# One order of 2311 operations replaced by another, in a kernel of decayed attention and a bilinear feed-forward block

## The chip, the core and the metric

The kernel runs on one core of a Trainium2 chip. The metric is the device time of one execution in microseconds (us). Three executions of the kernel before took 400.03, 401.91 and 403.84 us; their median, 401.91 us, is the time before.

## The reference

Eight batches of eight heads, 576 positions, 64 wide. Each head has causal attention in which a score gets a decay, the difference of two running sums of log f. The heads' outputs side by side are 4608 tokens of 512 values, which go through a bilinear block with a hidden width of 1536.

```python
scores = scale * np.matmul(q, k.transpose(0, 1, 3, 2))
cum = np.cumsum(np.log(np.clip(f, 0.0001, 1.0)), axis=-1)
decay = cum[:, :, :, None] - cum[:, :, None, :]
scores = np.where(causal, -1000000000.0, scores + decay)
attn = exp(scores - max) / (sum + 1e-09)
x = np.matmul(attn, v).transpose(0, 2, 1, 3).reshape(B * S, H * D)
out = ((x @ w_a) * (x @ w_b)) @ w_out
```

## The kernel before

The program first makes a list of 2311 operations; `op(engines, kind, function, deps)` adds one. An operation is a small group of instructions on one engine: E is TensorE, D is VectorE, A is ScalarE, P is GpSimd and S is the queue of SyncE, which issues transfers. Some operations may go to two or three engines ("DA", "APD"). Then `laid_out` sorts them by a list written out by hand of a search, `ORDER`, and gives each of the 278 that have a choice its letter from `CHOICE`. The loop at the end issues them in that order. So each engine works through its own part of `ORDER` strictly from front to back, and an operation that has to wait holds up all that stand behind it on its engine. How two operations of different engines stand to each other in `ORDER` counts only through the buffers: a pool's buffers are handed out in the order of the list.

The work falls into these kinds.

- **fill**: 40 operations of four 128x128 matmuls on an identity matrix, whose result nobody reads (line 178).
- **Inputs.** `ldqk` and `ldv` load q, k and v of a batch on S into a pool of three buffers (n32). `caqk` and `cav` cast them to 16 bits, and `tqk` (D, line 302) transposes q and k. For batch 0 the halves of q and k are loaded by operations 67 and 75 (k) and 71 and 79 (q); 83 and 84 load and cast the first rows of v. Operations 272 (k) and 275 (q) load the first halves of batch 1.
- **Decay.** `fclip`, `fln`, `fscan`, `fhi`, `flo` make the running sums, `crep` and `cev` spread them over partitions, and `stc` stores them (cum_d).
- **Weights.** `ldw` (line 365) are seven transfers issued by GpSimd: 89 and 90 are the first third of w_a and w_b (512 KB each), 91 and 92 the other two thirds (1 MB each), and 93 to 95 w_out.
- **Attention.** For two pairs of heads at a time: `qk0`, `qk1`, `qk3`, `qk2` (E, line 401) make scores; for batches 0 to 2 `max` (D, line 488) takes maxima, and for the rest `dec` (D, line 512) adds the decay and takes them; `exp` (A, lines 544 and 550), `rec` (D, lines 557 and 559), `norm` (P, line 567). The weights are then turned, in batch 0 by TensorE (`ptr`, line 591), later by a transposing transfer on S (`tr`, line 583), and `pve`, `pv` and `pv4` (E, lines 611 to 636) multiply them with v. The turned weights of rows 384 to 575 lie in a pool of two buffers, PTB: a `tr` into it waits until `pve`/`pv4` of two pairs of heads earlier have read theirs. Batches 0 and 1 are done with `pve` for rows 0 to 255 and for rows 256 to 511.
- **Feed-forward.** In 11 blocks of tokens: `psa` and `psb` (E, line 874), `aev` (A or D, casts psa), `mul` (D, line 890), `pso` (E, line 899), `ocopy` and `sto` (line 914). TensorE's list has these laid between the attention of later batches.

```python
RING = {"S": 2, "bc": 4, "n32": 3, "n16": 2, "PA": 3, "PB": 2, "PTA": 2, "PTB": 2, "st": 8, "ht": 15, ...}
```

Of the kernel before, what the change touches and what calls it, by code (L numbers as in the profile page):

```python
# [37 lines left out]
def kernel(  # L38
# [940 lines left out]
    for t0, n in [(0, 256), (256, 256), (512, 256), (768, 384)] + [(1152 + 512 * n, 512 if n < 6 else 384) for n in range(7)]:  # L979
# [3 lines left out]
        42-44 0 20 41 2 1 64 26 31 23 54 55 45 16 32 13 12 71 46 37 47 56 18 67 27 65 34 72 73 68 48 24 19  # L983
# [3 lines left out]
        142 6 154 155 92 147 143 159 149 91 148 144 160 162 161 108 166-168 145 172 131 52 53 132 179 173 14  # L987
# [42 lines left out]
        831 874 852 1880 875 1829 883 885 1883 1884 1000 884 841 1882 834 880 1885 911 854 857 886 1888-1890  # L1030
        882 814 858 859 849 890 856 891 812 887 912 835 855 1886 819 862 892 1891 864 860 889 888 823 863
        865 893 895 866 896 897 1893-1895 1898 914 881 861 902 898 899 959 960 1892 961 1899 1900 962 1887
        1896 926 927 1901 867 933 868 904 1001 966 934 903 894 901 900 1903 1904 1907 928-930 905 967-969
        1905 1908 813 1014 931 997 1906 815 1911 1909 1910 1912 970 1913 935 915 936 998 919 918 920 963 921
        922 1914 972 937 923 938 973 974 939 1007 940 975 932 971 941 1004 965 976 977 979 978 1915-1918
        1016 1018 1919 924 1921 943 947 916 964 1920 1002 942 994 1008 948 944 980 946 917 909 981 949 1922
        950 1923-1925 945 925 982 1019 952 954 953 1926 955 1015 983 956 913 1927 1928 1931 1932 951 1104
# [4 lines left out]
        1082 1052 1029 1084 1897 1953 1032 1088-1090 1956 1085 1195 1012 1055 1957 1958 1046 1197 1961 1010  # L1042
# [4 lines left out]
        1983 1985 1984 1986-1988 1160 1199 1113 1117 1118 1127 1128 1116 1216 1130 1120 1161 1214 1167 1133  # L1047
# [88 lines left out]
```

## Time and profile before

| | |
|---|---|
| median of three runs (lowest, highest) | 401.91 us (400.03, 403.84) |
| the profiled execution: span from the first to the last instruction | 400.7 us |
| mean granted clock of TensorE | 0.986 |
| busy: TensorE, VectorE, ScalarE, GpSimd | 383.2, 315.3, 250.0, 253.6 us |
| moved by the DMA engines | 78.22 MB |

The profile gives the profiled execution's span; what lies around it can be seen from the runs' median, which is 1.2 us above. PE in the profile is TensorE, DVE is VectorE, ACT is ScalarE, POOL is GpSimd and SP is SyncE (SPq its queue). A row of the timeline has the start, the time taken, the engine, the line, the operation and tiles, and in brackets how long the engine was idle before and what ended that. A row of a table by stretch has the busy time of each engine, then the granted clock of TensorE, the share of the DMA engines and the GB/s.

### The profile page before, as it was taken

Reading aid. Unit: us, or ns where it says so; the run is one execution under the profiler, and the core shown is the slowest. Engines: PE = TensorE matmul, PEld = TensorE weight load, DVE = VectorE, ACT = ScalarE, POOL = GpSimd, SP = SyncE. Lnnn points to the kernel's source line nnn. Section 1 sums busy time; section 2 is a strip of 40 time slices with the busy share of each in tenths; the row PEclk is TensorE's granted clock in tenths of the full one; section 3 lists DMA queues with packets and bytes.
Section 4 is the critical chain, followed back from the end, with each engine's and each line's share of the span. In section 5 each row is a group of like instructions: output and inputs, shape, how many; then the busy total and the mean of one; then the engine's idle time right before and its main releaser. Section 6 shows DMA issues by size and latency. Waiting matters only on the chain.

```text
span 400.7 us, 11076 instructions
## 1 busy us (share of the span) xinstructions
PE 383.2 (96%) x4040; PEld 212.0 (53%) x4040; DVE 315.3 (79%) x907; ACT 250.0 (62%) x757; POOL 253.6 (63%) x424
## 2 busy tenths in 40 slices
PE   8598799998999999999999999999999999999996
PEld 7466576765855544454445454544444444444553
DVE  8989798976778988997988889898969892373560
ACT  5798766666667778758785777577868673300011
POOL 3889876887397876897896849787968553000000
PEclk9889999998999999999999999999999999999999
DMA  7999989989999999999999999999997729000102
GB/s 282 240 186 289 204 177 224 213 150 215 208 301 208 227 171 330 201 277 212 295 187 286 211 255 273 233 241 190 276 187 218 157 66 202 28 2 36 71 0 79
DMA packets 148311, 78.22 MB, mean 195 GB/s; under 512 B 130592, under 2 KB 133408, under 8 KB 148256
## 3 DMA queue, kind: packets, MB, share of 16 engines
q1 hardware_dynamic: 144272, 72.53, 77.4%
q0 software_dynamic: 3696, 4.72, 7.0%
q8 instruction: 31, 0.51, 0.5%
q10 hardware_dynamic: 288, 0.26, 0.2%
q14 instruction: 24, 0.20, 0.1%
HBM read 49.69 MB, written 9.58 MB: 148 GB/s over the span
## 4 chain that ended last, share of the span: by engine, by line
PE 79%; DMA 9%; DVE 4%; POOL 2%; ACT 2%; issue 2%; SPq 0%; POOLq 0%; DVEq 0%; ACTq 0%
PE pso L899 22%; PE psa L874 22%; PE psb L874 21%; PE sc L401 8%; DMA wa<-in_moe_w_a_dram 5%; PE pv L611 2%; DVE st L488 2%; DMA k<-in_k_dram 1%; PE pv L613 1%; PE sc L636 1%; DMA PTB<-spread 1%; DMA PTB<-PB 1%; DVE qT L302 1%; PE pv L623 1%; ACT PB L550 1%
## 5 line engine op out<-in xcount | busy, mean ns | idle before, releaser
L874 PE MATMUL psa<-xT,wa 128*128 128x512 f16 (+2 forms) x528 | 116.2, 343 | 2.3 <-DMA wa<-in_moe_w_a_dram 1.7
L874 PE MATMUL psb<-xT,wb 128*128 128x512 f16 (+2 forms) x528 | 116.2, 343 | 0.1
L899 PE MATMUL pso<-wout,ht 128*128 128x512 f16 (+1 forms) x444 | 98.4, 374 | 0.0
L567 POOL TENSOR_SCALAR PA<-PA,st 128x128 f16<-128x128 f16 (+2 forms) x162 | 76.0, 482 | 31.8 <-DVE st L559 20.4
L890 DVE TENSOR_TENSOR ht<-psb,a 128x512 f16<-128x512 f32 (+2 forms) x132 | 76.2, 589 | 22.0 <-PE psb L874 15.0
L512 DVE CUSTOM_DVE_ANT_0 S<-sc,spread 128x128 f32<-128x128 f32 (+3 forms) x160 | 86.7, 567 | 7.7 <-PE sc L401 5.4
L138 ACT CAST a<-psa 128x512 f16<-128x512 f32 (+2 forms) x85 | 43.5, 515 | 55.9 <-PE psa L874 53.8
L874 PEld LDWEIGHTS <-wa 128*128 128x128 f16 x528 | 50.1, 99 | 45.5 <-issue 3.7
L874 PEld LDWEIGHTS <-wb 128*128 128x128 f16 x528 | 50.4, 99 | 41.5 <-issue 1.7
L567 POOL TENSOR_SCALAR PB<-PB,st 128x512 f16<-128x512 f16 (+1 forms) x84 | 58.7, 712 | 15.7 <-DVE st L559 14.6
L550 ACT ACTIVATE PA<-S,st 128x256 f16<-128x256 f32 (+2 forms) x120 | 59.9, 502 | 12.5 <-DVE st L512 12.4
L899 PEld LDWEIGHTS <-ht 128*128 128x128 f16 x444 | 41.7, 98 | 46.8 <-issue 1.3
L488 DVE TENSOR_REDUCE st<-sc 128x2 f32<-128x512 f32 (+7 forms) x68 | 46.3, 723 | 6.0 <-PE sc L401 5.3
L401 PE MATMUL sc<-kT,qT 32*128 32x128 f16 (+5 forms) x960 | 41.7, 272 | 5.5 <-ACT PA L550 2.1
L550 ACT ACTIVATE PB<-S,st 128x512 f16<-128x512 f32 x40 | 28.5, 714 | 7.9 <-DVE st L512 7.9
L401 PEld LDWEIGHTS <-qT 32*128 32x128 f16 (+1 forms) x960 | 18.6, 96 | 26.7 <-issue 14.4
L142 DVE CAST a<-psa 128x512 f16<-128x512 f32 (+2 forms) x47 | 26.2, 560 | 7.2 <-PE psa L874 6.6
L559 DVE RECIPROCAL st<-st 128x2 f32<-128x2 f32 x128 | 18.5, 157 | 14.0 <-ACT PA L550 8.7
L142 POOL CAST k<-k 128x1152 f16<-128x1152 f32 (+1 forms) x15 | 20.5, 1367 | 8.9 <-DMA k<-in_k_dram 8.9
L138 ACT COPY osb<-pso 128x512 f32<-128x512 f32 (+1 forms) x22 | 12.4, 570 | 19.9 <-PE pso L899 15.1
L138 ACT CAST xT<-pv 128x512 f16<-128x512 f32 (+2 forms) x39 | 17.0, 446 | 11.8 <-PE pv L636 5.8
L140 POOL TENSOR_SCALAR q<-q 128x1152 f16<-128x1152 f32 (+1 forms) x15 | 20.6, 1372 | 5.0 <-DMA q<-in_q_dram 4.2
(98 smaller groups left out, 491.5 us busy)
## 6 DMA issues: line engine op xcount, KB each, us to landing
spread<-cum_d SPq DMA_DIRECT2D x20, 576.0 KB, 5.9
out_dram<-osb SPq DMA_DIRECT2D x35, 256.0 KB, 3.8
q<-in_q_dram SPq DMA_DIRECT2D x15, 576.0 KB, 7.3
k<-in_k_dram SPq DMA_DIRECT2D x15, 576.0 KB, 5.2
v<-in_v_dram SPq DMA_DIRECT2D x32, 256.0 KB, 6.1
wout<-in_moe_w_out_dram POOLq DMA_DIRECT2D x3, 512.0 KB, 8.7
v<-in_v_dram SPq DMA_DIRECT2D x8, 128.0 KB, 7.2
wb<-in_moe_w_b_dram POOLq DMA_DIRECT2D x1, 1024.0 KB, 13.5
```

The costliest lines, as they stand in the source:

```text
L138: nc.scalar.copy(out=out_, in_=in_)
L140: ENG[e].tensor_scalar(out=out_, in0=in_, scalar1=0.125, scalar2=1.0, op0=MUL, op1=MUL)
L142: ENG[e].tensor_copy(out=out_, in_=in_)
L401: nc.tensor.matmul(out=dst, lhsT=lhsT, rhs=rhs, start=start, stop=stop, skip_group_check=True)
L488: nc.vector.tensor_reduce(out=m if i == 4 else st[:, 2 * i:2 * i + 2][:, h:h + 1] if isinstance(x, list) else m, in_=y, axis=AXX, op=MAX, ...
L512: nc.vector.tensor_tensor_reduce(out=o, in0=x, in1=y, scale=-1.0, scalar=3e38, op0=ADD, op1=MIN, accum_out=m)
L550: nc.scalar.activation(out=p_blocks(t, i)[:, :, h, :], in_=x.rearrange("p (j k) -> p j k", k=128), func=EXP, scale=sign, bias=st[:, c:c + ...
L559: nc.vector.reciprocal(out=st[:, 20 + 2 * i:22 + 2 * i], in_=st[:, 10 + 2 * i:12 + 2 * i])
L567: ENG[e].tensor_scalar(out=p, in0=p, scalar1=st[:, c:c + 1], scalar2=1.0, op0=MUL, op1=MUL)
L874: nc.tensor.matmul(out=o, lhsT=w16[:, db, 128 * fb:128 * fb + 128], rhs=tokens(db, t0, n), start=(db == 0), stop=(db == 3))
L890: nc.vector.tensor_tensor(out=ht[:, 0:n], in0=T.pop(("psb", t0, fb))[:, 0:n], in1=T.pop(("a16", t0, fb))[:, 0:n], op=MUL)
L899: nc.tensor.matmul(out=o, lhsT=T[("ht", t0, fb)][:, 128 * tb:128 * tb + 128], rhs=wout16[:, fb, c], start=(fb == 0), stop=(fb == 11))
```

## The change

`ORDER` and `CHOICE` are replaced; no operation, buffer or pool is added, removed or resized. 2214 of the 2311 places of `ORDER` hold another operation than before, but much of that is a shift. On TensorE the sequence of all `psa`, `psb` and `pso` is the same as before; of its 571 places 209 differ, through attention operations and `fill` that stand elsewhere. 105 operations change engine.

```diff
     ORDER = """
-        42-44 0 20 41 2 1 64 26 31 23 54 55 45 16 32 13 12 71 46 37 47 56 18 67 27 65 34 72 73 68 48 24 19
-        69 75 57 58 61 62 49 74 79 76 77 11 70 78 50 66 25 36 51 80 5 96 275 9 276 109 115 81 33 59 110 83
...
+        0 27 18 24 6 39 42 43 40 37 10 1 64 28 31 44-46 3 20 34 54 23 55 17 66 25 47 56 67 68 48 49 12 69 70
+        36 50 71 72 51 65 73 74 57 58 26 79-81 96 75 76 97 98 103 105 59 7 109 110 115 5 77 116 61 62 60 4
...
     CHOICE = """
-        DPAADDAAPPAPAAPADPADDAAADADDDDDAADDDDAAADAAADDAAAADAAAAADAAAAAADAAAAAADDAAADADADDAAAAAADDAAAAAAAAA
...
+        APDDAPAAPPAAPPPAAPPDDDAADDDAAADAADDADAAADAADAAAAAADDADDAAAAAAAADAAAADAAADADAAADDAAAAAADADAAADAADAA
...
```

Read engine by engine, the places on which the prediction rests are these (kind and number of the operation, in order):

```text
S before   ldf42 ldqk71 ldqk67 ldqk75 ldqk79 ldqk275 ldv83 ldv278 ldv85 ldqk272 ldv87 stc63 ldqk280 ...
S after    ldf42 ldqk67 ldqk71 ldqk79 ldqk75 ldv83 ldqk275 stc63 ldv85 ldqk272 ldqk280 ldv278 ldv87 ...
P before   const0 caqk72 caqk68 flo49 caqk77 pad66 caqk276 cav84 norm119 norm120 norm114 norm113 ldw89
           norm101 norm102 ldw90 norm107 cav279 norm138 ldw92 ldw91 ...
P after    const0 pad66 caqk68 flo49 caqk73 flo58 caqk76 caqk77 cav84 ldw89 norm120 norm119 ldw90
           norm114 norm113 caqk276 ldw91 (eight norms) ldw92 norm108 norm107 norm127 norm126 cav86 caqk273 ...
D before   ... fscan47 fscan56 fhi48 fhi57 flo58 tqk74 tqk70 tqk78 max109 max115 caqk81 tqk82 ...
D after    ... fscan47 fscan56 tqk70 cev51 tqk74 max97 max103 max109 max115 tqk82 tqk78 ... cev53 ...
E before   qk2 379, pv4 256, pv4 270, psa, fill, psb ... psa, qk0 464, pv4 426, pv4 417
E after    pv4 256, qk2 379, psa, psb, fill, pv4 270, psa ... psa, pv4 426, qk0 464, pv4 417
E before   pso, pve 424, pve 440, pve 422, pso, pso, qk3 466, pso x3, qk2 467, pv4 444, pve 431, pve 442
E after    pso x3, pve 424, pve 431, pve 440, qk3 466, pso x3, qk2 467, pv4 444, pve 422, pve 442
S before   ... tr438 tr437 ldv460 tr428 tr429 sto1655 tr439 tr430 ldqk603 tr526 ...
S after    ... sto1655 ldv460 tr428 ldv462 tr437 tr419 tr439 tr438 ldqk603 tr430 tr429 tr524 ...
```

`tr` 421 and 412 write the PTB buffers that `pv4` 426 and 417 read; `tr` 439 writes the one that `pv4` 444 reads, and waits for `pve` 424.

More of the change, by code (lines that the diff above doesn't have):

```diff
@@ L1032 @@
[L1032 to L1036, printed above, removed]
@@ new lines @@
+        317 1647 328 329 350 446 447 334 399 448 1648 1651 336 335 395 287 324 371 449 318 450 451 377 1652
+        319 1653 211 1654 330 331 396 1649 708 710 378 268 346 269 353 457 360 307 254 255 250 351 251 354
+        400 15 1656 1657 13 362 361 363 364 35 8 355 356 1660 458 1658 1661 313 325-327 1659 1662 1663 256
+        379 380 257 1664-1667 29 386 270 382 271 1668 1670 381 383 1669 1671 337 1672 1674 1673 1676 352
[3 rows of a table added]
+        1700 1702 1701 365 420 411 415 416 1703 465 480 1704-1706 508 320 481 424 1655 482 314 471 460 390
@@ new lines @@
+        456 391 332 339 483 510 509 511 338 428 431 333 462 437 499 440 441 432 477 466 384 514 515 486 487
+        1709-1711 459 467 419 516 425 488 409 1707 439 444 1712 422 423 453 490 518 624 438 442 443 445 1714
+        1716 492 491 493 1715 603 1718-1720 1722 385 405 519 430 520 506 1717 1721 463 358 500 1723 473 359
+        1724-1726 1728 472 1727 521 1729 429 433 434 528 540 435 436 541 1730 1732 546 548 547 1731 479 1734
+        1733 478 1736 1735 1738 1739 484 485 524 568 574 501 1737 1740 1742 1744 507 1743 517 1746 512 513
@@ new lines @@
+        526 569 575 576 489 1741 549 1748 1747 494 495 525 542 523 570 522 527 461 1749-1751 577 529 532 533
[4 rows of a table added]
+        671 679 673 678 566 567 672 1783-1785 589 596 639 595 680 645 674 675 598 1788 1789 1786 1790 594
+        681 609 640 647 1787 597 1792 682 1791 641 612 613 1793-1796 646 648 610 1798 1797 1800 1802 599 631
[3 rows of a table added]
+        616 661 662 666 665 667 625 697-699 628 1821 1822 1825 668 1826 716 700 701 800 658 761 769 663 1823
+        706 696 728 735 729 629 1771 669 730 737 731 763 762 764 1827 1828 1830 736 738 739 670 1831 704
@@ new lines @@
+        1832 1835 1837 1836 702 768 770 703 1838 615 802 617 771 803 772 1839 1840 705 717 707 721 724
+        732-734 1824 1841 741 720 718 719 773 725 1842 775 740 777 776 722 723 778 774 765 766 742 744 816
+        743 779 781 1843 1833 780 1844 1845 726 782 767 783 715 1847 745 746 749 750 1849 748 806 1848 807
+        1850 1846 1851-1853 784 1854 711 727 747 754 755 820 821 817 818 804 1855 1856 1859 751 752 1857 787
+        788 753 785 756-758 760 1861 1860 1862 1863 1858 824 869 790 789 791 836 837 844 1864 1867 1868 870
@@ new lines @@
+        1865 1866 759 786 808 792 793 1869-1871 1873 838 846 843 809 1872 876 1874 1834 810 877 1875 1876
+        811 1879 805 822 839-842 1877 1878 796 794 906 795 845 825 871 879 872-874 878 828 1881 847 849 797
+        826 829 814 815 832 848 830 831 833 850 851 853 883 884 999 1000 875 996 910 1829 1880 852 827 1883
+        907 885 880 881 854 855 1884 812 834 1882 1885 890 891 886 887 823 892 857 858 893 856 902 859
+        1888-1890 1886 860 835 819 862 864 1893 1894 1887 863 865 1895 1898 1899 895 897 1891 866 896 914
@@ new lines @@
+        898 899 926 933 934 928 888 882 889 904 911 1900 1903 1905 1904 1901 861 959 961 935 967 1892 927
+        966 929 1001 867 868 960 903 894 1906 968 1907 1908 901 1909 1911 1912 1896 1913 969 962 900 997 998
+        908 1910 813 915 918 930 932 905 1014 1016 919 963 964 922 1002 1914 936-938 920 921 970 923 1007
+        973 974 1915 931 939 1917 1018 940 941 976 975 977 1916 1919 1921 965 1918 942 943 1004 924 971
+        947-949 912 979 978 972 1920 1923 1015 944 1925 1924 909 980 916 917 946 981 950 1926 925 945 982
[4 rows of a table added]
@@ new lines @@
+        1028 1031 1048 1012 1025 1045 1050 1081-1084 1049 1078 1079 1051 1951 1952 1198 1953 1032 1080
+        1954-1956 1010 1957 1958 1006 1055 1052 1046 1040 1056 1017 1047 1085 1959 1961 1088-1090 1057 1054
+        1033 1021 1897 1029 1071 1199 1960 1106 1053 1100 1060 1061 1091 1072 1962 1963 1087 1109 1058 1093
+        1966 1967 1094 1062-1064 1112 1095 1124 1125 1131 1092 1073 1212 1086 1066 1096 1097 1099 1968 1971
+        1972 1126 1964 1132 1157 1165 1969 1102 1159 1167 1098 1065 1164 1166 1973 1975 1977 1133 1158 1160
@@ new lines @@
+        1976 1979 1059 1974 1978 1195 1110 1981 1980 1982-1984 1987 1988 1103 1127 1134 1011 1196 1985 1986
+        1013 1117 1120 1989 1128 1130 1101 1113 1116 1118 1161-1163 1129 1121 1168 1170 1202 1203 1990 1135
+        1136 1205 1206 1171-1173 1114 1138 1139 1991 1993 1992 1174 1175 1994 1122 1115 1145 1146 1140 1176
+        1141 1142 1144 1178 1970 1107 1995 1179 1119 1147 1148 1996 1999 1177 1997 2000 2003 1998 1965 1123
+        1111 2001 2002 1150 1151 2004 1180 1216 1218 1200 1217 2005 1183 1184 1152 1181 1153 1214 1154
@@ new lines @@
+        2007-2010 1143 2011 2012 1220 2006 1395 1137 2013 1186 1185 1187 1204 1169 1392 1265 1267 2014-2016
+        1149 1190 2017 2019 1272 2018 2020 2021 2024 1192 1266 1213 1232 1234 1156 1240 1233 1235 2025 2026
+        1155 1191 1207 1182 1189 1188 1274 1273 1239 1396 1397 1241 1221 1236 1237 1224 1193 1225 1226 2022
+        1201 1238 1228 1242-1245 2027 1229 1246 1268 1269 1271 1247 1275 1276 1278 1302 1248 1279 1280 2029
+        2030 1249 1281 1277 1250 1251 1282 1283 1285 1208 1284 2028 1222 1223 1270 1252 1303 1230 1286 1253
@@ new lines @@
+        1287 1219 1306 1307 1227 1288 1254-1257 2031 2034 2023 2035-2037 1231 1298 1289 2032 1291 1293 1292
[10 rows of a table added]
+        1423 1504 1399 1474 1476 1407 1422 1500 1467 1469 1424-1427 1444 1475 1477 1479 1478 2096 1468 2099
[7 rows of a table added]
+        1569 1532 1574-1576 1571 2140 2143 2145 1572 2144 2147 1541 1542 2142 1577 2146 1533 1503 1519 1546
[3 rows of a table added]
+        2179 2180 2183 2181 2182 2184-2187 2189 2188 2191 2193 2190 2192 2195 2197 2194 2196 2199 2159 2198
+        2201 2200 2202 2203 2205 2204 2207 2209 2208 2211 2210 2174 2213 2212 2214-2217 2219 2218 2220 2221
@@ L1086 @@
+        2206 2223 2222 2224-2226 2228-2237 1594 1597 1588 1591 2238-2240 2243 2244 2247 2245 2246 2249 2248
+        2250 2251 2253 2241 2252 2255 2254 2256-2260 2263 2261 2262 2264 2265 2267 2266 2227 2269 2268
+        2271-2273 2275 2276 2270 2277 2278 2274 2242 2279-2284 2287 2288 2285 2291 2292 2286 2289 2290 2293
+        2296 2294 2295 2297 2298 2301 2299 2300 2302-2310
     """
     CHOICE = """
-        DPAADDAAPPAPAAPADPADDAAADADDDDDAADDDDAAADAAADDAAAADAAAAADAAAAAAADAAAAAADDAAADADADDAAAAAADDAAAAAAAAA
@@ L1089 @@
-        AAADDDAADADDAAAADDADDDDDADAADDADDADADAAAADAAADADAADAAAADAAAAAADDDAAAAAADADAAAAAAADAADAAAAAADAAAAADA
-        AADAAADADAAADAADAAAAAAAAAADDAAADAAADDAAAAAADAAAAADDADDDDDADDDDADDDDAADADDDAADAAA
+        APDDAPAAPPAAPPPAAPPDDDAADDDAAADAADDADAAADAADAAAAAAADDADDAAAAAAAADAAAAADAAADADAAADDAAAAAADADAAADAADAA
+        DDDDAAAADDDDADADDDAADDAADDDDDADDDADDADDDADDDAADDDDAAAAAAAAAAADAADAAADAAAAADAAADAAAAAAAAADDDAAAAAAAAD
+        DDAAAADDADAAAAAAAAAAAAAAADADAADAADAAAAAADADAADDDADAAADDDDDDADDDDADAAADAAAADAAS
```

33 lines of the change are left out of this document (3 added, 30 removed), and 109 rows, old and new, of the table ORDER.

## The prediction

> **What bounds the kernel now.** I read the page first, then tables by stretch, then the waits of TensorE, and then the timeline around each wait.
>
> ```profile
> span 400.7 us, 11076 instructions
> ...
> PE 383.2 (96%) x4040; PEld 212.0 (53%) x4040; DVE 315.3 (79%) x907; ACT 250.0 (62%) x757; POOL 253.6 (63%) x424
> ...
> PE   8598799998999999999999999999999999999996
> ```
>
> TensorE is busy for all but 17.5 us of the span. Since the change leaves its operations alone, what can be won is idle time, half-clock time and small stalls. The last row has TensorE's busy tenths in 40 slices of 10 us: from the eleventh on each digit but the last is a 9. There the new list can win little, and can lose. The tables by stretch say where these lie.
>
> ```profile
> 8.00:20.00 12.00, 6.67 (x151) 4.87 (x151) 11.62 (x25) 8.38 (x33) 10.20 (x22) 0.88 0.99 265
> 20.00:32.00 12.00, 11.05 (x178) 8.29 (x176) 10.44 (x25) 9.89 (x35) 10.16 (x18) 0.83 1.12 196
> 32.00:44.00 12.00, 8.85 (x174) 6.74 (x172) 11.44 (x31) 10.19 (x35) 11.01 (x16) 1.00 1.10 277
> 44.00:78.00 34.00, 33.76 (x554) 24.88 (x558) 30.91 (x69) 23.88 (x75) 25.20 (x40) 1.00 1.01 204
> 92.00:106.00 14.00, 11.78 (x199) 9.52 (x192) 8.16 (x20) 8.78 (x30) 8.58 (x13) 0.88 1.16 201
> ```
>
> The columns after the length are PE, PEld, DVE, ACT, POOL, clock, DMA share. From 8 to 44 us VectorE is the fullest engine (33.50 of 36), and TensorE waits. So the case is decided in the first 106 us, by these waits:
>
> ```profile
> PE sc L401 <- ACT PA L550: 2.1, 1, 2.1
> PE sc L401 <- DVE st L559: 2.1, 1, 2.1
> PE pv L636 <- DMA PTB<-spread: 1.8, 1, 1.8
> PE psa L874 <- DMA wa<-in_moe_w_a_dram: 1.7, 1, 1.7
> PE pv L636 <- DVE st L488: 0.8, 1, 0.8
> ```
>
> The first two are score matmuls ahead of 20 us that wait for the softmax to give up their buffers. They are not all recoverable, since VectorE is full there.
>
> **The first 20 us.** VectorE loses three pieces of work and gains one:
>
> ```profile
> 6.99 0.49 DVE L142 CAST wout<-cum_f 32x256 f16<-32x256 f32 x2
> 7.52 1.03 DVE L220 TENSOR_TENSOR wout<-cum_f,wout 32x320 f16<-32x320 f32 x1
> 12.65 1.16 DVE L140 TENSOR_SCALAR q<-wout 128x512 f16<-128x512 f32 x1
> 28.95 0.40 DVE L142 CAST xT<-pv 128x256 f16<-128x256 f32 x1
> ```
>
> The two fhi go to ScalarE (0.49), flo 58 to GpSimd (1.03), the cast 81 of q to ScalarE (1.16); both cev of 256 columns come to VectorE, whose nearest row is the cast at 28.95 (0.40 each). Net 0.49 + 1.03 + 1.16 - 0.80 = 1.9 us less on the fullest engine. ScalarE and GpSimd have the room (8.38 and 10.20 of 12). **I count 1.9 us**; the bounds are 0, if another queue takes over, and 4.2, both waits.
>
> **The weights.** The 1.7 us are the wait for the second part of w_a:
>
> ```profile
> 14.43 1.04 POOL L142 CAST nv<-v 128x1024 f16<-128x1024 f32 x1 [0.90 <-DMA v<-in_v_dram]
> 17.05 0.98 POOL L365 DMA_DIRECT2D wa<-in_moe_w_a_dram  x1
> 22.51 0.75 POOL L365 DMA_DIRECT2D wa<-in_moe_w_a_dram  x1
> 22.51 21.65 DMA wa<-in_moe_w_a_dram
> 44.21 0.61 PE L874 MATMUL psa<-xT,wa 128*128 128x256 f16 x4 [1.65 <-DMA wa<-in_moe_w_a_dram]
> ```
>
> It is issued last of four at 22.51 and lands 21.65 us later. From 20 to 32 us the two queues shared the transfer engines thus:
>
> ```profile
> q0 software_dynamic: 1505, 1.97, 98.1%
> q1 hardware_dynamic: 625, 0.35, 13.5%
> cum_d<-cum_f SPq DMA_DIRECT2D x1, 144.0 KB, 11.0
> ```
>
> GpSimd's queue had 98% of them and moved 1.97 MB in 12 us; SP's small store of the sums took 11.0 us. In the new list w_a's second part goes ahead of w_b's, two norms and a cast after ldw 90. Also v is loaded before batch 1's q, into the third free buffer, so cast 84 needn't wait till 14.43 and the first issue comes up to 4 us sooner. At 1.97 MB in 12 us the 2.1 MB up to its end take 12.8 us: counted from 20 us it lands near 33 instead of 44. w_b's second part, now last, needs 6.4 us more at that rate, 13 if SP's queue takes half: 39 to 46, less up to 4 for the sooner start, against the 42.6 (44.21 - 1.65) at which TensorE asks now and 40.7 with the gain above. **I count 1.65 us**; bounds 0 and 1.65. It is hidden again if GpSimd's norms ahead of the issues come late.
>
> The Trainium skill ("DMA: Bandwidth & Descriptors", the section on queues, rings and completion order) says that each engine goes round the queue rows packet by packet; even shares would make about 21 us of the 2.1 MB (half of the 2.3 MB that all queues moved in 12 us), so w_a's second part would land at 41 and w_b's after it. The 98.1% against 13.5% speak against even shares here, though SP had little queued; the sum above goes by the row.
>
> **The transposes.** The 0.8 us are laid to VectorE, but the wait is for a transposing transfer. Below are the chain, SP's queue from 69 us on, the landings of these two transposes and of all, and TensorE:
>
> ```profile
> 66.43 0.44 PE psa L874 x4
> 68.68 1.08 PE sc L401 x26
> 69.76 0.43 PE pv L636 x20
> ...
> 70.19 6.36 SPq L583 DMA_TRANSPOSE PTB<-PB  x2
> ...
> DMA to landing us min/median/max: 6.0/6.4/6.9
> ...
> DMA to landing us min/median/max: 2.8/4.4/7.2
> ...
> 78.27 0.35 PE L636 MATMUL pv<-PTB,nv 128*64 128x64 f16 x10
> 79.45 0.35 PE L636 MATMUL pv<-PTB,nv 128*64 128x64 f16 x10 [0.84 <-DVE st L488]
> ```
>
> pv4 256 and 270 free both buffers at 70.19; tr 421 and 412 are issued at 70.2 and 73.4 (half of 6.36 later) and land 6.9 and 6.0 us later, at 77.1 and 79.4. The second is the 0.84. TensorE's work between the release and pv4 426 was 78.27 - 70.19 = 8.1 us. The new list moves qk2 379, a psa, a psb and a fill (1.08 + 0.44 + 0.44 + half a psa = 2.2 us) from behind the release of pv4 256 to before that of 270, for which tr 421 now waits: the lead shrinks to 5.9. With the same landings the first waits 1.0 and the second (9.2 us after the release, wanted after 7.0) 2.2 in all instead of 0.84. With the median landing of 4.4 neither waits. **I count 0.5 us lost**, bounds 1.4 lost and 0.84 won.
>
> ```profile
> 84.96 4.37 SPq L583 DMA_TRANSPOSE xT<-spread  x2
> 90.06 3.54 SPq L583 DMA_TRANSPOSE PTB<-spread  x2
> 90.06 4.18 DMA PTB<-spread
> ...
> 85.60 0.28 PE L623 MATMUL pv<-PTB,nv 128*64 128x128 f16 x4
> 86.14 1.90 PE L899 MATMUL pso<-wout,ht 128*128 128x512 f16 x8
> 94.28 0.35 PE L636 MATMUL pv<-PTB,nv 128*64 128x64 f16 x10 [1.77 <-DMA PTB<-spread]
> 96.00:98.00 2.00, 2.00 (x11) 1.39 (x10) 1.01 (x3) 1.62 (x6) 0.76 (x2) 0.50 0.71 233
> ```
>
> The 1.8 us come from order in SP's queue: pve 424 frees the buffer at 85.9, but tr 439 stands behind tr 428, tr 429 (4.37 together) and a store and is issued at 90.06; it lands 4.18 later. The new list puts it before 429, with the store long gone. TensorE's work between 424 and 444, 92.5 - 85.9 = 6.6 us, loses two pso (1.73 at the rate of the row at 86.14): 4.9. Issued at once, a landing of 4.18 fits; tr 438, now behind it, is wanted after a pv4 and a pve more, some 0.7 us later, and lands 1.6 (half of 3.54, rounded down) + 4.4 = 6.0 after the release, 0.4 late. **I count 1.4 us won**, bounds -1.5 (two landings of 6.9) and 1.8.
>
> After that gap the clock is 0.50 for 96 to 98 us; the stretch of 92 to 106 has 0.88 of 14 us, so 3.4 us ran at half, which costs 1.7. **I count half, 0.85**, since any 1.5 us gap may bring it back. The Trainium skill ("TensorE: Matmul & The Clock Gate", the section on oscillation) allows idle gaps up to about 3.4 us without throttling; by it, closing this gap would win no clock. The trace differs: 1.77 us sufficed. The half clock in 16 to 24 us I count at nothing: TensorE isn't the bound there (bounds 0 and 2).
>
> Last, tr 527 waits for pv4 435, which now stands behind qk0 528, a psa and a psb (about 0.9 + 0.44 + 0.44 = 1.8 us less lead; no wait shows there now): **0.3 lost**, bounds 0 and 1.5.
>
> **Sum.** 1.9 + 1.65 - 0.5 + 1.4 + 0.85 - 0.3 = 5.0, so a span of 395.7. The runs' median lies 1.2 above the span: 396.9. The last store goes by SP in place of ScalarE, which I leave in the rounding. I forecast **397.0**. The head start of 44 us must be kept until 120: from 44 to 78 us VectorE has 3.1 us of room and GpSimd 8.8, which hides it.
>
> **Rivals.** *Transposes as tight as before* (0.27): the first 44 us win their 3.5, but 421/412, 439 and 527 wait with congested landings, 1.4 + 0 + 1.0 lost and the half clock kept: 400.7 - 3.5 + 2.4 + 1.2 = 400.8; with one of them free 399.5, which I take. For it: the leads shrink in three of four places. Against it: 439's queue is cleared.
>
> *The early gain is not kept* (0.14): VectorE is as full with other work, or GpSimd, which takes flo 58, more casts and waits for caqk 276 ahead of ldw 91, delays the norms by as much; only 439 and the clock change: 400.7 - 1.4 + 0.8 + 1.2 = 401.3.
>
> *Slower* (0.11): the sooner weights starve SP's loads of batch 1. cav 86 and caqk 273 stand right behind ldw 92 on GpSimd, which comes to them near 25 us (22.5 and four norms). If k's load takes the 11 us of cum_d and goes out once the weights flow, at some 17 to 22, it lands at 28 to 33, and all norms of batch 0 that stand behind, which feed the transposes and TensorE, are 3 to 8 us late. Of that 3.5, the early gain gone and one more half-clock window (1.7) give 400.7 + 3.5 + 1.7 + 1.2 = 407, and 405 if 439 still wins. It decides from an issue at about 14 us on (25 - 11).
>
> *Even shares of the two queues* (0.03): w_a's second part lands at 41 and w_b's later, TensorE waits there as now, and the 1.65 fall away: 398.6. This is what the page named above would give.
>
> **Numbers.** The forecast has the remaining 0.45; its own range is 393.5 to 399. Runs of 400.0 to 403.8 say that a change under 1% (4 us) can't be told from none. Below 397.9 lie 0.36 of the forecast's 0.45 and the better end of the first two rivals, 0.10 (leads that suffice after all): faster 0.46. Slower is 0.12, the slower case and a little of the second. The rest, 0.42, is within 1%. The range of 393.5 to 403 leaves out most of the slower case and a tail of some 0.08 at the fast end.
>
> **What would show it.** Right: the first psa waits no more for wa at about 40 us; TensorE's two waits for score buffers shrink to some 2.3 us together; no gap over 1 us at the pv4 near 75 and 90 us; fewer half-clock windows. Wrong: a wait for PTB over 1.5 us; a GpSimd cast waiting for k near 25 us; any idle of TensorE after 120 us, where I assume that the new list keeps it as busy as now.

## The result, and the profile after

The changed kernel takes **406.07 us** (median of 14 runs, 405.11 to 408.35) against 402.20 us before (14 runs, 400.03 to 404.28). The ratio is **1.0107, with a 95% interval of 1.0084 to 1.0130**: it is 4.3 us slower. The prediction said 397.0, and its range ended at 403.0.

The page of the changed kernel has, for the rows shown of before:

```profile
span 404.0 us, 11033 instructions
...
PE 384.1 (95%) x4040; PEld 212.3 (53%) x4040; DVE 314.0 (78%) x911; ACT 248.9 (62%) x750; POOL 254.5 (63%) x427
...
PE   6698899998999999999999999999999999999996
...
PEclk9559999999999999999999999999999999999999
```

The span is 3.3 us longer. TensorE's idle time is 19.9 us instead of 17.5, and its clock is near half in the second and third slice. In the stages that the prediction used, and in the rest of the attention work (for the changed kernel first, then for the kernel before; the columns are again length, PE, PEld, DVE, ACT, POOL, clock, DMA share and GB/s):

```profile
8.00:20.00 12.00, 6.38 (x135) 4.26 (x133) 8.17 (x20) 9.47 (x30) 7.47 (x12) 0.67 1.10 268
20.00:32.00 12.00, 10.98 (x164) 8.31 (x164) 11.45 (x26) 10.18 (x39) 9.58 (x18) 0.62 1.11 228
...
44.00:78.00 34.00, 32.43 (x539) 24.54 (x539) 29.43 (x68) 26.38 (x81) 27.77 (x42) 1.00 1.07 213
...
92.00:106.00 14.00, 12.91 (x213) 9.86 (x211) 12.32 (x31) 8.75 (x31) 10.28 (x17) 1.00 1.11 181
...
sum 231.00, PE 226.85 PEld 112.06 DVE 197.49 ACT 161.22 POOL 168.59; mean PE 37.81 PEld 18.68 DVE 32.91 ACT 26.87 POOL 28.10
```

```profile
sum 231.00, PE 230.50 PEld 114.42 DVE 199.56 ACT 167.90 POOL 173.32; mean PE 38.42 PEld 19.07 DVE 33.26 ACT 27.98 POOL 28.89
```

Four things are to be read. From 8 to 20 us VectorE has shed 3.5 us (11.62 to 8.17), and TensorE did not become busier for it. From 44 to 78 us TensorE lost 1.3 us of work, from 92 to 106 us it gained 1.1. And in the 231 us from 99 to 330, which the two sums cover, TensorE was idle for 0.5 us before and is for 4.15 now. TensorE's waits say with whom (total, times, longest):

```profile
PE sc L401 <- DVE kT L302: 2.3, 1, 2.3
PE sc L401 <- DVE qT L302: 1.8, 1, 1.8
PE sc L636 <- DMA PTB<-PB: 1.6, 3, 0.8
PE psP L591 <- DVE xT L142: 1.6, 1, 1.6
...
PE pv L623 <- DMA xT<-spread: 1.3, 2, 1.0
...
PE pso L899 <- DMA wout<-in_moe_w_out_dram: 0.8, 1, 0.8
```

All five waits quoted of before are gone, w_a's 1.7 and the 1.8 at `pv4` 444 among them. Others stand in their place.

TensorE's FFN sequence is the same in both kernels, so the start of its k-th matmul instruction (of 1500) measures progress. The table gives the length of the stages in us, worked out from these starts, with lowest and highest of all profiles taken in this study whose code up to the end of the stage is that of the order (of the rear: whose code in the stage is that order's, whatever the front). The lists of e4 and e16 change at FFN matmul 0, so they count in the last row alone; e18, edited near matmul 224 and beyond, counts in the first two.

| stage, to FFN matmul | profile before | profile after | old order, all | new order, all |
|---|---|---|---|---|
| the start, to 0 | 30.4 | 31.8 | 30.4 to 31.2 (5) | 31.5 to 32.6 (7) |
| 0 to 48 | 17.4 | 16.4 | 16.6 to 19.3 (5) | 16.4 to 16.5 (7) |
| 48 to 224 | 39.3 | 39.4 | 38.7 to 39.3 (5) | 39.4 to 39.9 (6) |
| 224 to 260 | 12.4 | 10.1 | 10.0 to 12.4 (4) | 10.1 to 13.3 (3) |
| 0 to 260 together | 69.1 | 65.8 | 65.9 to 69.1 (4) | 65.8 to 69.1 (3) |
| the rear, 260 to 1160 | 230.2 | 235.4 | 230.1 to 233.5 (8) | 235.1 to 237.3 (4) |

Two stages carry the loss, the start with 1.4 us (means 30.6 and 32.0) and the rear with 4.5 us (means 231.6 and 236.1). The rear has the same 2244 matmul records in both orders, so its lengths compare like with like. The three stages between do not: the new list moves eleven `ptr` matmuls from 0 to 48 into the next stage, and 26 of `pve` from there into 224 to 260. Taken together they hold the same work but for four matmuls of fill, and there the means are equal, 67.2 us. The two losses add up to 5.9 us where the runs differ by 4.3; the profiles are few. From 1160 to the last matmul it is 67.5 us in both. The last column but one also shows that the profile of before, on which the sum was built, was a slow one here: it had 12.4 us in a stage that took 10.0 to 11.0 in the three other executions of the same code, and the longest of the four lengths from 0 to 260.

### The profile page after: what moved, and what is told of

It is laid out like the page before. It is cut to its first block, busy times and chain, and to the rows that moved or that the text cites. A ratio compares the mean times of both kernels' runs of the same rounds, so it can differ in the third digit from the quotient of the medians.

```text
span 404.0 us, 11033 instructions
## 1 busy us (share of the span) xinstructions
PE 384.1 (95%) x4040; PEld 212.3 (53%) x4040; DVE 314.0 (78%) x911; ACT 248.9 (62%) x750; POOL 254.5 (63%) x427
## 4 chain that ended last, share of the span: by engine, by line
PE 60%; DMA 11%; DVE 10%; POOL 9%; ACT 4%; issue 4%; SPq 1%; POOLq 0%; ACTq 0%
PE psa L874 17%; PE psb L874 16%; PE pso L899 15%; PE sc L401 6%; DVE st L488 4%; DMA spread<-cum_d 3%; POOL PA L567 2%; DVE S L512 2%; DMA PTB<-PB 2%; PE pv L611 2%; POOL spread L567 2%; DMA k<-in_k_dram 2%; POOL PB L567 1%; DMA xT<-spread 1%; DMA q<-in_q_dram 1%
## 5 line engine op out<-in xcount | busy, mean ns | idle before, releaser
L567 POOL TENSOR_SCALAR PA<-PA,st 128x128 f16<-128x128 f16 (+2 forms) x162 | 75.1, 478 | 42.5 <-DVE st L559 29.1
L138 ACT CAST a<-psa 128x512 f16<-128x512 f32 (+2 forms) x80 | 41.6, 525 | 34.4 <-PE psa L874 32.1
L488 DVE TENSOR_REDUCE st<-sc 128x2 f32<-128x512 f32 (+8 forms) x68 | 46.6, 726 | 12.3 <-PE sc L401 8.0
L142 DVE CAST a<-psa 128x256 f16<-128x256 f32 (+2 forms) x52 | 27.5, 536 | 6.0 <-PE psa L874 5.4
L559 DVE RECIPROCAL st<-st 128x2 f32<-128x2 f32 x128 | 18.6, 157 | 14.1 <-ACT PA L550 9.0
L550 ACT ACTIVATE PA<-sc,st 128x256 f16<-128x256 f32 (+2 forms) x42 | 19.5, 476 | 9.7 <-DVE st L488 9.1
L142 POOL CAST nv<-v 128x1024 f16<-128x1024 f32 (+1 forms) x24 | 21.3, 892 | 3.5 <-DMA v<-in_v_dram 3.5
## 6 DMA issues: line engine op xcount, KB each, us to landing
wa<-in_moe_w_a_dram POOLq DMA_DIRECT2D x1, 1024.0 KB, 11.5
```

The source lines that it names most:

```text
L138: nc.scalar.copy(out=out_, in_=in_)
L142: ENG[e].tensor_copy(out=out_, in_=in_)
L488: nc.vector.tensor_reduce(out=m if i == 4 else st[:, 2 * i:2 * i + 2][:, h:h + 1] if isinstance(x, list) else m, in_=y, axis=AXX, op=MAX, ...
L550: nc.scalar.activation(out=p_blocks(t, i)[:, :, h, :], in_=x.rearrange("p (j k) -> p j k", k=128), func=EXP, scale=sign, bias=st[:, c:c + ...
L559: nc.vector.reciprocal(out=st[:, 20 + 2 * i:22 + 2 * i], in_=st[:, 10 + 2 * i:12 + 2 * i])
L567: ENG[e].tensor_scalar(out=p, in0=p, scalar1=st[:, c:c + 1], scalar2=1.0, op0=MUL, op1=MUL)
```

## The experiments

Apart from the edits shown, all kernels have the same operations. "Old" and "new" are the orders with their choices of engines. Ratios are against the kernel before, with 95% intervals.

**One part alone: w_a's load ahead of w_b's.**

```diff
-        142 6 154 155 92 147 143 159 149 91 148 144 160 162 161 108 166-168 145 172 131 52 53 132 179 173 14
+        142 6 154 155 91 147 143 159 149 92 148 144 160 162 161 108 166-168 145 172 131 52 53 132 179 173 14
```

> The order before, with one thing of the change: the load of the second third of wa (operation 91) stands ahead of that of wb (92) in GpSimd's stream. The wait of 1.65 us for wa at 42.56 should be gone. Theory (the next late arrival takes the place of the wait, as the changed kernel's wait of 1.60 us at 43.16 suggests): the time stays within 0.6 us of before, 401.6 to 402.6. Rival (the forecast's own step, a wait removed is kept to the end): 1.65 us less, 400.5.

Measured: 0.9997 (0.9971 to 1.0023). The wait is gone; of TensorE's waits between 31 and 46 us only 0.3 us concern a weight:

```profile
PE psb L874 <- DMA wb<-in_moe_w_b_dram: 0.3, 1, 0.3
```

The stage 0 to 48 took 16.1 us, and yet the time is the same within 1.2 us (the interval's lower end). The rival's 1.65 us, kept to the end, are outside the interval.

**Front and rear exchanged.** The seam is at FFN matmul 256, operation 1722; in the last kernel at the first one, operation 1598.

```text
e2: new up to 1722, then what is left in the old order      e3: old up to 1722, then what is left in the new order
e4: new up to 1598, then what is left in the old order
```

> The new order up to matrix multiplication 256 of the FFN (start at 98.9 us before, 1.7 us sooner in the changed kernel), then every remaining operation in the old order with the old engines. Theory (the front of the new order gains, its rear loses): the lead of 1.8 us is kept by the old rear, 400.4. Rival (the rear is slow because of what the front leaves behind, late loads and full buffers): no gain is kept, 402 to 406.

> The old order up to the same matrix multiplication, then the rest in the new order. Theory (the rear of the new order loses 5.2 us by itself, from a lead of 1.8 to a lag of 3.4): 402.2 + 5.2 = 407.4. Rival (the rear is harmless behind the old front): 402.2. In between, 404.0, if a part of the rear's loss is only the lead of operations that the new front had drawn ahead of the cut.

> The new order up to the first matrix multiplication of the FFN (30.4 us before, 31.8 after), then the old order. Theory (the new start costs 1.5 us and nothing behind makes up for it): 402.2 + 1.5 = 403.7; its load of wa comes early, so that with that wait's 1.65 us kept it would be 402.0. Rival (the start carries the whole loss, by its half-clock stretch of 17 us and the loads it delays): 405 to 406.

Measured: 1.0113 (1.0070 to 1.0157), 1.0088 (1.0056 to 1.0119) and 1.0215 (1.0183 to 1.0247). The rear alone loses 3.5 us, between the theory's 5.2 and its in-between value. But the new front alone loses 4.5 us instead of gaining 1.8, so the first theory falls; in its profile 2.3 us are lost ahead of FFN matmul 260 and 2.2 behind it. The two kernels lose 8.0 us together, not the 4.3 of the whole, so a seam probably costs something of its own. In e4 one wait of 6.4 us stands behind it, and that kernel tells nothing more.

**The start: engines alone, and everything but the engines.**

```diff
 # e5: ORDER old; in CHOICE nine letters new       # e6: ORDER new; the same nine letters old
-fhi48 D  fhi57 D  flo58 D  caqk81 D  caqk76 A  caqk72 P  caqk73 A  cev51 A  cev53 D
+fhi48 A  fhi57 A  flo58 P  caqk81 A  caqk76 P  caqk72 A  caqk73 P  cev51 D  cev53 A
```

> The order before, with the new engines for nine operations of the start alone: casts 48, 57 and 81 from VectorE to ScalarE, 58 from VectorE to GpSimd, 76 from ScalarE to GpSimd, 72 and 73 exchanged between GpSimd and ScalarE, copies 51 and 53 exchanged between ScalarE and VectorE. The forecast's step (VectorE is the bound of the first 20 us): the first FFN multiplication up to 1.9 us sooner than 30.4 us and a time of 400 to 401. Theory from the changed kernel's trace (the second halves of q and k now come late from ScalarE and GpSimd, the first product with them starts at 16.60 instead of 15.18 us): 1.5 us more, near 403. Nothing measurable, if the new order is needed for either: 401.6 plus or minus 1.

> The new order, with the same nine operations on their old engines. Theory (these engines cost the new start its 1.5 us): 406.0 - 1.5 = 404.5, and a half-clock stretch shorter than 13 us. Rival (the order of the start costs it, not the engines): unchanged, 406. The forecast's step (the new engines gain 1.9 us): slower than the changed kernel, 408.

Measured: 0.9986 (0.9955 to 1.0017) and 1.0233 (1.0178 to 1.0288). In the old order the new engines make the first FFN matmul 1.9 us later (32.5 us against the mean of 30.6), the opposite of the forecast's step: VectorE waits for GpSimd's cast of k, which now stands behind `flo` 58.

```profile
11.49 1.21 DVE L302 STREAM_TRANSPOSE kT<-k 128x576 f32<-128x576 f32 x1 [1.94 <-POOL k L142]
```

The wait for w_a is then missing from TensorE's waits, and the time is the same: w_a lands at 44.6 us here and at 44.2 before, and a weight that lands so late absorbs a late start just as it absorbs an early one. In the new order the old engines are 5 us worse, and the first FFN matmul comes at 35.1 us; there the forecast's step has its sign, and more than its size. So the order alone makes the start later than 30.6 us, the engines alone do too, and together they partly make up for each other.

**The rear: which queue?**

```text
e7: old front; rear of VectorE, ScalarE, GpSimd, SyncE new, of TensorE old      e8: old; only TensorE's rear new
```

> The old order up to FFN multiplication 256 (98.9 us); behind it the new order and engines of VectorE, ScalarE, GpSimd and SyncE, with TensorE's own order left as before. Theory (the rear loses because the maxima, exponentials, normalisations and transposes that feed TensorE come later in their queues): the loss of 3.5 us of the run with the whole new rear stays or grows, 405 to 407. Rival (TensorE's own new order puts its attention work too early): 401.6, as before.

> The old order and engines everywhere, with TensorE's order alone new from FFN multiplication 256 up to 1240 (the last attention work). Rival theory (TensorE's new order is what loses): the 3.5 us of the whole new rear, 405. Theory (the queues of the other engines lose): 401.6, or 402.5 if single products that were moved ahead now wait.

Measured: 1.0242 (1.0191 to 1.0293) and 1.0101 (1.0048 to 1.0155). TensorE's new order alone, behind 99 us, loses what the whole new rear loses (the rear took 234.9 us). The other queues' new order alone loses more. TensorE's waits from 98 to 330 us in e8 are short and have several partners; the longest are these:

```profile
PE sc L636 <- DMA PTB<-PB: 1.0, 2, 0.6
PE sc L401 <- DVE st L512: 0.8, 1, 0.8
PE psa L874 <- DVE a L142: 0.7, 2, 0.5
```

**The rear's single waits, moved away.** TensorE's list alone is edited; old with the swap of e1 in e10.

```diff
 # e9, new order; the same for 433, 631, 1024, 1423
-psb1751 pv4 529 pv4 533 psa1754 qk1 537 psb1755
+psb1751 pv4 529 psa1754 psb1755 pv4 533 qk1 537
 # e10, old order
-pv4 426 pv4 417 psb1689 fill psa1692        qk2 467 pv4 444 pve 431 pve 442 fill fill
+pv4 426 psb1689 psa1692 pv4 417 fill        qk2 467 pve 431 pve 442 fill fill pv4 444
```

> The new order, with five attention products of TensorE's order (433, 533, 631, 1024, 1423: those that wait in the profile at 100, 108, 131, 215 and 301 us, for 0.98, 0.83, 0.56, 0.62 and 0.23 us, mostly for transposes that SyncE has issued 1.4 to 3.6 us before) each put behind two more FFN multiplications. Theory (the rear loses by these single waits, since the transposes land just behind the product): they go, 3.2 us less, 403. Rival (each wait only shows that VectorE, ScalarE and GpSimd are behind as a whole, and comes back at the next product): unchanged, 405.5 to 406.5.

> The old order with the load of wa ahead of that of wb, as before in the swap alone, and with the same edit at its own waits: product 417 (a wait of 0.84 us at 78.61) behind two more FFN multiplications, product 444 (1.78 us at 92.50) behind two other products and two fills that are ready, its eviction moved behind theirs. Theory (a wait that goes is kept, since behind 99 us TensorE hardly waits): 1.0 for the swap, 0.8 and 1.2, 3.0 us in all, 398.7. Rival (given back at the next late buffer, as with the swap alone): 401 to 402.

Measured: 1.0176 (1.0150 to 1.0202), and 0.9983 (0.9961 to 1.0006). Both theories fall. e10's rival holds; e9 is 2.8 us slower than the changed kernel, which its rival did not expect either. In e9 no product waits for PTB any more, but the score products do, for VectorE's maxima to free their buffers, and the rear took 238.9 us:

```profile
PE sc L401 <- DVE st L512: 2.4, 4, 1.1
```

In e10 both old waits are gone; w_b, now last, keeps TensorE for 3.0 us, and another transpose for 1.1:

```profile
PE psb L874 <- DMA wb<-in_moe_w_b_dram: 3.0, 1, 3.0
PE pv L623 <- DMA PTB<-spread: 1.1, 1, 1.1
```

**The half clock of the start.**

```diff
-        for n in range(4):
+        for m in range(LONG.get(n, 4)):    # e11, old order with the swap: LONG = {21: 32}; e12, new order: {26: 28, 2: 36}
```

> The old order with the load of wa ahead of that of wb, and the fill ahead of the first products of batch 0's second heads (operation 21) longer by 28 small multiplications, which occupy the wait of 2.12 us at 13.06. Theory (the half-clock stretch of 6.8 to 10.2 us behind it costs the start): it goes or shrinks, the first FFN multiplication comes 1 us sooner and the swap lets it be kept: 400.5. Rival (TensorE waits for VectorE's casts and maxima there at any clock): 401.6, no change against before.

> The new order with two fills made longer (26 by 24 small multiplications, 2 by 32), in front of the waits of 1.82 us at 8.12 and 2.32 us at 14.28. Theory (the half-clock stretch of 17 us from 12 us on is what delays the new start by 1.5 us): it shrinks to 7 us or less, the first FFN multiplication starts near 30.4 instead of 31.8 us, 404.5. Rival (the start waits for late casts at any clock): the stretch shrinks and the time stays, 406; if the fills outlast the waits, up to 407.

Measured: 1.0044 (1.0020 to 1.0068) and 1.0063 (1.0035 to 1.0091). In the old order neither expectation holds: the half-clock stretches of the start are 10.2 us in all (6.8 before), the first FFN matmul comes at 32.9, and the time is 1.8 us more. In the new order, from 8 to 20 us, the clock is 0.97 instead of 0.67:

```profile
8.00:20.00 12.00, 8.07 (x196) 6.67 (x194) 8.81 (x21) 10.01 (x33) 7.47 (x12) 0.97 1.09 264
```

The half-clock stretch is 10.2 us instead of 17.1, the first FFN matmul starts at 31.4 (mean of the new order 32.0), and the ratio is 0.0044 below the changed kernel's, 1.8 us. The two intervals overlap a little, so this is likely but not certain.

**VectorE and ScalarE made lighter.** e13 and e15 leave the second FFN product out of all but 32 columns, e14 leaves out half of the first, and e17 half of the hidden values.

```diff
 # e13 (new) and e15 (old), tokens from 512 on; q = 32
-tensor_tensor(out=ht[:, 0:n], in0=psb[:, 0:n], in1=a16[:, 0:n])
+tensor_tensor(out=ht[:, 0:q], in0=psb[:, 0:q], in1=a16[:, 0:q]); tensor_tensor(out=ht[:, q:n], in0=a16[:, q:n], in1=a16[:, q:n])
 # e14 (new): the copy out of psa at n // 2 columns          # e17 (new): the multiplication at half its columns
```

> The new order, with VectorE's multiplications of the FFN lightened from the third block of tokens on (token 512 and above, from 97 us on): only the first 32 columns multiply the PSUM product with its partner, the other columns square the fp16 copy, which leaves the second FFN product out of the result and shortens an instruction of 0.68 us. Theory (the rear's waits come from VectorE's queue being late): the waits behind 99 us shrink from 5.4 us to under 1.5, 402. Rival (they come from GpSimd's normalisations and SyncE's transposes): unchanged, 406.

> Control: the old order with the same light multiplication as in the new one. TensorE waits 0.5 us in all behind 99 us there, so that nearly nothing can be gained: 401.5 to 402.3. If it gains 3 us or more, VectorE's length is worth that much in any order, and the run of the new order says nothing about its rear.

> The new order, with the FFN's copies out of PSUM (most of them on ScalarE) at half their columns from token 512 on; the multiplication reads that half twice, so that half of the first FFN product is left out of the result. Theory (VectorE's queue is late, ScalarE's is not): 405, since 12 of the copies in 200 us are VectorE's. Rival (ScalarE's exponentials come late, behind its copies, and VectorE's reciprocals wait for them, 12.4 us of its idle time against 8.8 before): most of the rear's loss goes, 402 to 403.

> The new order, with VectorE's FFN multiplications at half their columns from token 512 on (the third FFN matrix multiplication reads that half for all rows, so that half of the hidden values is left out of the result): a copy of 256 columns out of PSUM took VectorE 0.41 us where the multiplication of 512 took 0.68, so about 17 us less of VectorE's work between 120 and 320 us. Theory (VectorE's queue is what is late in the rear): TensorE's waits behind 99 us, 5.4 us by its starts, fall under 2, and the time is 402 to 403. Rival (transposes in SyncE's queue and GpSimd's normalisations): the waits stay, 405.5 to 406.5.

Measured: e13 1.0186 (1.0147 to 1.0224), e15 1.0063 (1.0034 to 1.0091), e14 1.0123 (1.0081 to 1.0165), e17 1.0133 (1.0091 to 1.0174). The light multiplication was a heavy one, on the mean 182 + 599 ns instead of 684 (from 120 to 320 us, e15):

```profile
L893 DVE TENSOR_TENSOR ht<-a 128x480 f16<-128x480 f16 x53 | 31.8, 599 | 0.0
L891 DVE TENSOR_TENSOR ht<-psb,a 128x32 f16<-128x32 f32 x65 | 11.8, 182 | 4.4 <-PE psb L874 3.1 <-ACT a L138 0.2
```

So the pair tells what 0.1 us more per multiplication costs: 2.5 us in the old order, and 3.2 on top of the new one's loss. The Trainium skill ("VectorE: DVE Perf Modes", the perf-mode tier table) gives a two-input operation of 16-bit data in SBUF twice the rate. The trace agrees for those that ran while GpSimd was idle: 480 columns took 377 to 399 ns. The mean of 599 comes from some that ran beside GpSimd's work and took up to 1590; the last section has both. e17 is shorter for certain:

```profile
L891 DVE TENSOR_TENSOR ht<-psb,a 128x256 f16<-128x256 f32 x53 | 21.7, 419 | 5.9 <-PE psb L874 3.0 <-ACT a L138 2.2
```

That takes 14 us of work off VectorE in these 200 us (53 times 0.265). The rear took 234.2 us, 1.2 less than the changed kernel's profile, and the time is that of the changed kernel within its interval. Lighter copies change nothing that can be seen either. Set against the changed kernel's ratio, the two intervals leave room for a gain of at most 0.9 us (e17) and 1.3 us (e14), so the amount of VectorE's multiplications or ScalarE's copies is not what most of the new rear's 4.5 us come from.

**The middle alone, and one transpose put back.**

```diff
 # e16: old up to 1598, new up to 1722, old behind it
 # e18, new order, SyncE:                                      GpSimd: cav 463 behind the norms 358 and 359
-tr437 tr419 tr439 tr438 ldqk603 tr430 tr429 tr524
+tr437 tr419 tr429 tr439 tr438 ldqk603 tr430 tr524
```

> The old order up to the first FFN multiplication (30.4 us), the new one from there to FFN multiplication 256 (98.9 us), the old one behind it. Theory (the middle gains a little, by the traces so far 0.75 us up to multiplication 48 and 0.55 from 224 to 260, and loses 0.4 between): 401.4. Rival (the middle carries the front's loss, by its new waits at 43 and 60 us): 404 to 406. A seam between two schedules can cost something of its own, as the 6.4 us wait of the run with the new start alone: this would show as one long wait just behind 30 or 98 us.

> The new order, with transpose 429 put back ahead of 439, 438 and 430 in SyncE's queue, as it stood before the change, and GpSimd's cast 463, which waits 3.47 us for a load of v at 85.5, behind the normalisations 358 and 359 that feed 429. Theory (SyncE issues without a break there, so that a wait only changes its place): the wait of 0.98 us at product 433 goes and one of 0.7 to 1.8 us comes back at product 444, and the time stays within 0.7 us of the changed kernel, 405.4 to 406.8. The forecast's step (the new place of 439 gains 1.4 us for good): 407.5. Rival (the cast's wait for v was what made 429 late, and order has nothing to do with it): both products are free of waits, 405.

Measured: 1.0068 (1.0039 to 1.0097) and 1.0207 (1.0167 to 1.0246). e16 reached FFN matmul 260 at 98.4 us, within the 96.3 to 99.4 of the old order, and its rear took 233.5 us, the longest of the old order's; TensorE's longest waits behind the seam are for transposes:

```profile
PE pv L623 <- DMA xT<-spread: 1.1, 1, 1.1
PE pv L623 <- DMA PTB<-spread: 1.0, 1, 1.0
```

In e18 the wait came back at product 444 as expected, yet the other did not quite go, and the clock fell to half behind it:

```profile
96.42 0.35 PE L636 MATMUL pv<-PTB,nv 128*64 128x64 f16 x10 [1.64 <-DMA PTB<-spread]
...
103.64 0.25 PE L623 MATMUL pv<-PTB,nv 128*64 128x128 f16 x2 [0.40 <-DMA PTB<-spread]
```

It is 4.0 us slower than the changed kernel by the ratios, so the theory of an exchange without loss falls, and so does the rival, by which the cast's wait for v made 429 late: with that cast moved away, GpSimd waits at the same place for VectorE,

```profile
89.55 0.93 POOL L567 TENSOR_SCALAR PA<-PA,st 128x256 f16<-128x256 f16 x2 [4.22 <-DVE st L559]
...
91.06 1.21 SPq L583 DMA_TRANSPOSE xT<-spread  x1
92.37 1.50 SPq L583 DMA_TRANSPOSE PTB<-spread  x1
```

and SyncE stands still until 91.06 for the norms of `tr` 429, with `tr` 439 behind it (88.46 in the changed kernel). So in the new order the new place of 439 is worth having, and the forecast's sign holds there. The size is not shown: the 4.0 us hold the move of the cast and the half clock behind the gap as well.

No kernel here beats the one before by more than its interval; e10, at 0.9983, comes nearest.

## Why the prediction was wrong, point by point

**The first 20 us (1.9 won; measured 1.4 lost).** The step summed VectorE's work as if it were the bound. VectorE did get lighter, by 3.5 us, and then stood idle, waiting for ScalarE. One of the two waits that it quotes was also misread: the product at 15.18 in the kernel before came right behind VectorE's transpose of q, which it needs and whose row runs from 13.92 to 15.13, and not behind a score buffer. This is the chain of work that leads to the score product of batch 0's second heads in the changed kernel (start, length, engine, tile):

```profile
7.69 0.88 ACT q L136
8.59 0.61 ACT L202
...
10.09 0.35 ACT wout L138
10.43 1.41 ACT q L136 x2
11.85 0.46 ACT PA L550 x2
12.33 1.03 DVE st L488 x2
13.38 0.57 ACT PA L550 x2
13.98 0.42 DVE st L488
14.40 1.11 DVE qT L302
15.51 1.04 DVE kT L302
16.60 1.40 PE sc L401 x38
```

L202 is the second table load, for the exponential. It took 1.28 us (its row is below) and stands ahead of the cast `fhi` 57 and two casts of q, so that the first exponential begins at 11.75 us. On VectorE the new list has four maxima ahead of the last two transposes, where the old one had two maxima ahead of the last alone, and the maxima wait 0.86 and 0.63 us for exponentials. So the transposes come late, and the product stands at 16.60 against 15.18 before. In the kernel before, the table was loaded ahead of all casts. The load in the changed kernel, then in the kernel before:

```profile
8.59 1.28 ACT L202 ACT_TABLE_LOAD   x1
...
4.90 1.28 ACT L202 ACT_TABLE_LOAD   x1
```

ScalarE "has the room (8.38 of 12)" was true as a share and irrelevant. No run moves the table load or the maxima alone, so how the 1.4 us divide between them is not shown; e5, which loads the table at 4.93 and starts the FFN late all the same, shows that another link can be as slow. One term was also too large: the 1.16 us for the cast 81 of q are a row with GpSimd at work beside it, and in e6 the same cast took VectorE 0.41.

The half clock, counted at nothing in the early start (bounds 0 and 2), is 6.8 to 10.2 us long in the first 30 us of the profiles with the old start and 13.7 to 17.1 us with the new one; e12 prices the part that its fills remove at about 1.8 us, of which 0.5 shows at the first FFN matmul.

**w_a's wait (1.65 won; the wait went, the gain did not come).** The mechanism was right up to the landing: GpSimd issued the load at 20.87 us, it landed 11.5 us later, at 32.4 (the forecast had near 33), and TensorE no longer waits for it. But the sum took a wait that goes for time that is won. In the same stage TensorE now waits as long for a copy by VectorE,

```profile
44.76 0.61 PE L591 MATMUL psP<-ident,PB 128*128 128x128 f16 x8 [1.60 <-DVE xT L142]
```

and its idle time between FFN matmuls 0 and 48 fell only from 3.4 to 3.0 us. The rest by which that stage is shorter is work that the new list does later (14.1 us of matmuls before, 13.3 now). e1 shows that the wait alone is worth nothing measurable.

**`tr` 421 and 412 (0.5 lost).** Neither `pv4` waits now: 0.84 was won, its better bound, if the profile of before is the measure; in three more executions of the old front the wait was 0.75, 0.48 and 0.50 us.

**`tr` 439 and the clock behind it (1.4 + 0.85 won).** In the two profiles compared, this came true (12.4 to 10.1 us). It was mis-sized by taking one execution for the kernel: in three more executions of the old front the wait at 444 was 1.33, 1.38 and 0.46 us and no half clock followed, and e2, with the new front, has a half-clock window near 92 us. TensorE's idle time in the stage is 1.6 us on the mean of four profiles with the old front and 1.0 of three with the new one, so some 0.5 us were won there, and over 0 to 260 nothing. And the wait went on to `pve` 433, for `tr` 429, which now stands last:

```profile
100.09 0.25 PE L623 MATMUL pv<-xT,nv 128*64 128x128 f16 x2 [0.98 <-DMA xT<-spread]
...
108.30 0.35 PE L636 MATMUL sc<-PTB,nv 128*64 128x64 f16 x10 [0.83 <-DMA PTB<-PB]
```

**`tr` 527 (0.3 lost).** The second row: 0.83, inside its bounds.

**Nothing lost behind 120 us (measured about 3.1 lost there, 4.5 from 99 us on).** This term, put at nothing, is the largest error. From FFN matmul 372, at 122 us, to 1160 the old order took 207.8 to 210.2 us (8 profiles, mean 208.8) and the new one 210.8 to 212.4 (4, mean 211.9). The dense rear of the old list was read as a property of the work; it is a property of the list. e3 loses 3.5 us with the new rear alone. e8 shows that TensorE's new order alone suffices for that, and e7 that the other queues' new order does not suit TensorE's old one. e9, e14 and e17 speak against three simple causes: five badly placed products, ScalarE's copies, the length of VectorE's multiplications. What stays open is which of TensorE's moved products begins it: the waits are 0.2 to 1.0 us each, on several partners, and moving five of the products only led to other waits.

**The rivals.** By its number "slower" (407, or 405) was the nearest, by luck: its mechanism was loads starved by the weights, and no cast waiting for k near 25 us shows. By mechanism "the early gain is not kept" was nearer, with 401.3 and a chance of 0.14; but it laid the blame on VectorE or GpSimd, and it still counted 439's gain. Of the signs that the prediction named, w_a's wait, the gaps near 75 and 90 us went its way; the score waits (1.8 and 2.3) did not shrink, the half-clock stretches grew, and TensorE is idle after 120 us, its own sign of being wrong.

## What to carry to other kernels

A stage that is full to the last microsecond is not safe from a new order: price a rewritten list there as a loss with a bound, not as zero. A busy share does not say what a freed engine is worth; follow the chain of the first late operand through each engine's queue, table loads included. When two orders are compared by stages, count the work in each stage first. Before a wait of one profiled execution enters a sum, ask whether another execution of the same code shows it, and what lands next if it goes.

## What the runs showed of the hardware that I had not expected

The half-clock stretches come in steps of 3.41 us (6.8, 10.2, 13.7 and 17.1 us in these profiles) and begin elsewhere in each execution of the same code: at 17.2, 16.2, 15.6 and 17.4 us in four profiles of the old start. Of the same new front, e2's profile has 0.89 and 0.54 where the changed kernel's has 0.67 and 0.62:

```profile
8.00:20.00 12.00, 6.04 (x143) 4.04 (x141) 8.11 (x19) 9.54 (x29) 7.26 (x12) 0.89 1.06 250
20.00:32.00 12.00, 10.89 (x138) 8.28 (x141) 11.55 (x27) 10.28 (x39) 10.03 (x18) 0.54 1.10 238
```

The Trainium skill ("TensorE: Matmul & The Clock Gate", Part 1) speaks of a free-running window of that length, and the trace agrees. Near 92 us, gaps of 0.46, 1.33, 1.38 and 1.45 us were followed by no half clock, those of 1.64 and 1.77 us by 3.4 us of it. Length alone does not decide: gaps of 1.60, 1.65 and 1.70 us near 44 us were followed by none, and in e2 two gaps of 0.93 and 0.82 us within 2.1 us were followed by a window. The same page's section on oscillation, by which gaps up to 3.4 us cost no clock, does not hold here.

A product of VectorE with both operands in SBUF depends on what GpSimd does beside it. In e15 (fp16, the same tile twice) those that ran while GpSimd was idle took 257 to 267 ns for 224 columns, 323 to 332 for 352 and 377 to 399 for 480, about 0.52 ns for each added column. Of 480 columns, those that overlapped GpSimd's work took 391 to 1590 ns, with a median of 479. Two of them, with GpSimd's row beside the first; at 349 us GpSimd is idle:

```profile
277.79 1.40 POOL L142 CAST k<-k 128x1152 f16<-128x1152 f32 x1
277.95 1.50 DVE L893 TENSOR_TENSOR ht<-a 128x480 f16<-128x480 f16 x1
...
349.04 0.40 DVE L893 TENSOR_TENSOR ht<-a 128x480 f16<-128x480 f16 x1
```

The kernel's own multiplication, with one operand in PSUM, took 664 to 693 ns for 512 columns in the kernel before, GpSimd busy or not, and 1.02 ns for each added column (553 for 384 and 684 for 512).

The Trainium skill ("ScalarE: Activation LUTs", the section on table sets) says that a logarithm followed by an exponential needs one table load, since one set has both. The traces show two here, the one at 0.73 us for the logarithm and the one that the new list put at 8.59.
